# Moving a sketched linear attention and its MLP to 32x32 vector transposes, eight-tile float32 rounds, column-tiled kv and a list scheduler

## The chip, the cores and the metric

The kernel runs on one core of one Trainium2 chip. The metric is the device time of one execution in microseconds (us). The span that a profile shows is about 2 us shorter than the device time of the same run. The record calls a run slow when it is over 1.5% above the fastest of its kernel.

Engine names in the profiles: PE is TensorE's matmuls, PEld its weight loads, DVE is VectorE, ACT is ScalarE, POOL is GpSimd, SP is SyncE. A name with a q behind it (ACTq, SPq) is the engine's sequencer, which also issues DMAs.

## The reference

There are 4 batches, 4 heads, a sequence of 1088 and a head size of 32, so 4352 tokens of width 128. The MLP has 2048 hidden units.

```python
def phi(x):                                   # S1, S2: 8 x 32
    a = einsum('rd,bhsd->bhsr', S1, x)        # 8 numbers per token and head
    b = einsum('rd,bhsd->bhsr', S2, x)        # 8 more
    return outer(a, b).reshape(..., 64)       # 64 features
q_p, k_p = phi(q), phi(k)
kv  = einsum('bhsf,bhsd->bhfd', k_p, v)       # 64 x 32 per batch and head
z   = k_p.sum(axis=2)                         # 64 per batch and head
x   = (q_p @ kv) / (q_p . z + 1e-6)           # 4352 x 128
h   = x @ w_in                                # 128 x 2048
g   = maximum(h, 0) + alpha * minimum(h, 0)
out = g @ w_out                               # 2048 x 128
```

Both kernels rewrite the activation in the same way. Since min(h, 0) = h - relu(h), the output is x W + relu(h) w_a, with w_b = alpha * w_out, w_a = w_out - w_b and W = w_in w_b. These three are made on the chip once, after the weights have landed. So the first output matmul waits for w_in and w_out, and for a GpSimd product and difference.

## The kernel before

Everything except the hidden layer (bf16) is float32. A sequence of 1088 is 1024 plus a rest of 64, and rests of several batches are packed together. Work is written as short lists of steps. A merge by estimated cost interleaves the MLP of one batch with the queries of the next and the keys of the one after, and this fixes each engine's order.

```python
    def load_main(t, src, b):                  # one head at a time: 128-byte pieces
        for h in range(H):
            nc.sync.dma_start(t[:, :, h], bass.AP(..., ap=[[NJ * D, 128], [D, NJ], [1, D]]))
    ...                                        # cut: every load is issued by SyncE
    def k_feat(src, nj, ptag, store, abtag=None):
        ...                                    # transposes by TensorE, copy to kT
            nc.vector.tensor_mul(kp[:, :n], ...)         # outer product: VectorE, PSUM x SBUF
    ...
        def kv(kp_chunk, vt, rows, first, last):         # k features stationary, v moving
            for p in range(2):                           # two heads and the ones for z: 96 columns
                nc.tensor.matmul(acc["ps"][:, p], kp_chunk[rows, 2 * p:2 * p + 2]...,
                                 vt[rows, 3 * p:3 * p + 3], ...)
    ...
    def q_steps(srcs, col0, parts, ptag):      # half a batch: 512 tokens
        def tr():                              # four TensorE transposes, then a copy to qT
        ...
        def feat(S_):                          # two tiles (64 rows each) at once
            for p in range(2):
                nc.tensor.matmul(ps[:, p, :n], S_[64 * p:64 * (p + 1)]...,
                                 s["qT"][64 * p:64 * (p + 1), :n], start=True, stop=True)
        ...                                    # fa: Sa, copied by ScalarE; fb: Sb, multiplied by VectorE
        def nd():                              # two tiles at once, denominators, then numerators
            for o in (1, 0):
                for (b, c0, nn) in parts:
                    for p in range(2):
                        nc.tensor.matmul(ps[64 * p:64 * (p + 1), o, c0:c0 + nn], ...)
```

## Time and profile before

| | before |
|---|---|
| device time, median of 5 runs beside the changed kernel | 182.47 us (181.14 to 184.46) |
| span of the profiled run | 179.3 us |
| first hidden-layer matmul | 54.9 us (its own record is missing; its weights are loaded at 54.71) |
| last start on TensorE | 173.6 us |

These lines are from the page of the kernel before: the span, busy time with share and number of instructions per engine, then busy tenths in 40 slices of the span (9 is 90% or more), the clock that TensorE was granted in tenths, DMA rate per slice, and the shares of the chain of work that ended last.

```profile
span 179.3 us, 2240 instructions
...
PE 150.5 (84%) x817; PEld 82.9 (46%) x828; DVE 83.7 (47%) x152; ACT 79.6 (44%) x149; POOL 17.0 (9%) x35
...
PE   0160099999599999999999999999999999999970
...
GB/s 38 186 115 195 343 228 116 94 220 162 213 56 4 2 0 0 0 62 2 0 0 59 4 0 59 0 0 0 61 1 0 59 0 0 62 0 62 0 59 29
...
PE 79%; SPq 7%; DMA 5%; ACT 3%; DVE 2%; issue 2%; ACTq 0%
```

TensorE is full from the twelfth slice on (a slice is 4.5 us), and nothing else is near full. The first eleven slices are different: there the loads run, TensorE has holes, and no output is made. The table of windows of the kernel before says the same in numbers. Its columns are the window in us, its length, busy us (and instructions) of PE, PEld, DVE, ACT and POOL, the granted clock, the DMA share and GB/s.

```profile
0.00:20.00 20.00, 3.67 (x12) 2.29 (x12) 2.70 (x21) 2.32 (x4) 2.95 (x18) 1.00 0.71 155
20.00:40.00 20.00, 17.32 (x124) 16.12 (x124) 4.84 (x7) 5.58 (x11) 14.04 (x17) 1.00 0.89 187
...
80.00:100.00 20.00, 19.89 (x114) 11.18 (x114) 11.24 (x17) 10.93 (x20) 0.00 (x0) 1.00 0.04 15
```

In 80 to 100 us TensorE is busy 19.89 of 20 us, VectorE and ScalarE about 11. In the chain of waits of the kernel before (start, length, what), the longest single piece is the transfer of w_in:

```profile
14.44 8.18 DMA w_in_f<-in_moe_w_in_dram
```

What the parts to be changed cost is read from the timeline of the kernel before (start, length, engine, line, output<-inputs, shapes, count):

```profile
37.95 1.13 PE L308 MATMUL ps_w_339<-qT,Sa 64*128 64x512 f32 x4
...
43.79 1.94 PE L330 MATMUL ps_nd<-qp,kz_322 128*64 128x512 f32 x8
...
82.20 1.92 PE L261 MATMUL ps_kvz<-v_78,kp 128*128 128x96 f32 x16
```

A feature round of half a batch is one pair of tiles with 512 float32 columns in 1.13 us (recorded as four instructions, two per float32 matmul). Numerators and denominators take 1.94 us, and half of a batch's kv takes 1.92 us.

### The profile page before, as it was taken

The page shows a single profiled execution, that of the slowest core. Times are in us where ns is not written, and L with a number is a line of the kernel's source. Part 1 is how long each engine was busy: PE and PEld are TensorE (multiplying, and loading weights), DVE is VectorE, ACT ScalarE, POOL GpSimd, SP SyncE. Part 2 cuts the span into 40 slices and gives each one's busy share as a digit, 9 for nine tenths or more (in the row PEclk, how much of TensorE's full clock was granted, in tenths as well). Part 3 has the DMA queues.
Part 4 walks back from the last instruction along what each step waited for, and adds up shares of the span by engine and source line. Part 5 has one row for each costly group of instructions (what it writes and reads, how often), then busy time and mean ns, then how long its engine had stood idle before and what let it go on. Part 6 is the DMA issues. An engine that isn't in the chain of part 4 may idle for free.

```text
span 179.3 us, 2240 instructions
## 1 busy us (share of the span) xinstructions
PE 150.5 (84%) x817; PEld 82.9 (46%) x828; DVE 83.7 (47%) x152; ACT 79.6 (44%) x149; POOL 17.0 (9%) x35
## 2 busy tenths in 40 slices
PE   0160099999599999999999999999999999999970
PEld 0030099965263545456454554633333434355540
DVE  3010052115623662764558185454656647757740
ACT  2010051051126761755376285535635657657540
POOL 6000499600000000000000000000000000000000
PEclk9999999999999999999999999999999999999998
DMA  2968997599930000010001001000100100101011
GB/s 38 186 115 195 343 228 116 94 220 162 213 56 4 2 0 0 0 62 2 0 0 59 4 0 59 0 0 0 61 1 0 59 0 0 62 0 62 0 59 29
DMA packets 41050, 11.16 MB, mean 62 GB/s; under 512 B 37056, under 2 KB 39376, under 8 KB 40912
## 3 DMA queue, kind: packets, MB, share of 16 engines
q1 hardware_dynamic: 41040, 11.03, 27.4%
q8 instruction: 6, 0.10, 0.3%
q14 instruction: 4, 0.03, 0.1%
HBM read 8.80 MB, written 2.23 MB: 62 GB/s over the span
## 4 chain that ended last, share of the span: by engine, by line
PE 79%; SPq 7%; DMA 5%; ACT 3%; DVE 2%; issue 2%; ACTq 0%
PE ps_h L360 16%; PE ps_o L373 16%; PE ps_kvz L261 10%; PE ps_nd L330 9%; PE ps_ab L235 5%; DMA w_in_f<-in_moe_w_in_dram 5%; SPq L90 3%; PE ps_ot L391 3%; PE ps_qt L300 2%; PE ps_w L212 2%; PE ps_wt L203 2%; PE ps_kt L226 2%; DVE kp L243 1%; PE ps_o L372 1%; SPq L116 1%
## 5 line engine op out<-in xcount | busy, mean ns | idle before, releaser
L364 ACT ACTIVATE rh<-ps_h 128x512 bf16<-128x512 f32 (+1 forms) x98 | 53.5, 582 | 38.5 <-PE ps_h L360 35.9
L360 PE MATMUL ps_h<-xT,w_in_bf 128*128 128x512 bf16 (+1 forms) x139 | 48.6, 367 | 0.6 <-issue 0.2
L373 PE MATMUL ps_o<-rh,w_a_bf 128*128 128x512 bf16 (+1 forms) x138 | 47.3, 366 | 0.2
L366 DVE TENSOR_SCALAR rh<-ps_h 128x512 bf16<-128x512 f32 (+1 forms) x46 | 29.5, 647 | 14.6 <-PE ps_h L360 12.9
L360 PEld LDWEIGHTS <-w_in_bf 128*128 128x128 bf16 x144 | 14.2, 99 | 21.9 <-issue 11.9
L373 PEld LDWEIGHTS <-w_a_bf 128*128 128x128 bf16 x144 | 14.1, 98 | 14.4 <-issue 4.0
L335 DVE STREAM_TRANSPOSE dt<-ps_nd 128x512 f32<-128x512 f32 (+1 forms) x9 | 6.2, 687 | 18.2 <-PE ps_nd L330 18.2
L243 DVE TENSOR_TENSOR kp<-ps_ab,b_sb 128x1024 f32<-128x1024 f32 x8 | 9.8, 1224 | 9.4 <-ACT b_sb L75 9.4
L203 PE MATMUL ps_wt<-ident,w_in_f 128*128 128x128 f32 x16 | 3.9, 397 | 9.5 <-DMA w_in_f<-in_moe_w_in_dram 9.5
L235 PEld LDWEIGHTS ps_ab<-S12blk,kT 128*128 128x128 f32 x68 | 9.5, 211 | 5.1 <-ACT kT L75 2.8
L235 PE MATMUL ps_ab<-S12blk,kT 128*128 128x64 f32 x68 | 10.6, 298 | 1.0 <-ACT kT L75 1.0
L75 ACT COPY kT<-ps_kt 128x512 f32<-128x512 f32 (+1 forms) x9 | 4.7, 522 | 14.7 <-PE ps_kt L226 14.7
L196 POOL TENSOR_SCALAR w_b_f<-w_out_f,S12T_165 128x128 f32<-128x128 f32 x16 | 9.5, 616 | 16.7 <-DMA w_out_f<-in_moe_w_out_dram 16.7
L77 DVE COPY oT<-ps_ot 128x512 f32<-128x512 f32 (+1 forms) x8 | 5.3, 658 | 10.8 <-PE ps_ot L391 10.8
L203 PEld LDWEIGHTS ps_wt<-ident,w_in_f 128*128 128x128 f32 x16 | 3.0, 216 | 10.0 <-DMA w_in_f<-in_moe_w_in_dram 9.9
L75 ACT CAST w_in_bf<-w_in_f 128x512 bf16<-128x512 f32 x3 | 1.7, 615 | 10.7 <-DMA w_in_f<-in_moe_w_in_dram 10.7
L75 ACT COPY qT<-ps_qt 128x512 f32<-128x512 f32 (+1 forms) x9 | 5.2, 573 | 2.7 <-PE ps_qt L300 2.7
L340 DVE STREAM_TRANSPOSE rr<-rc 128x512 f32<-128x512 f32 (+1 forms) x9 | 6.1, 682 | 0.3
L75 ACT COPY b_sb<-ps_ab 128x128 f32<-128x128 f32 (+1 forms) x10 | 2.5, 251 | 7.9 <-PE ps_ab L235 7.9
L391 PE MATMUL ps_ot<-ident,ob 128*128 128x128 f32 x34 | 5.6, 281 | 0.5 <-ACT ob L75 0.5
L261 PE MATMUL ps_kvz<-v_77,kp 128*128 128x96 f32 x32 | 4.3, 282 | 2.0 <-DVE kp L243 2.0
L341 DVE TENSOR_TENSOR xT<-ps_nd,rr 128x512 bf16<-128x512 f32 (+1 forms) x9 | 5.9, 653 | 0.1
(148 smaller groups left out, 170.8 us busy)
## 6 DMA issues: line engine op xcount, KB each, us to landing
out_dram<-oT SPq DMA_DIRECT2D x8, 256.0 KB, 2.0
w_in_f<-in_moe_w_in_dram SPq DMA_DIRECT2D x1, 1024.0 KB, 8.2
k_68<-in_k_dram SPq DMA_DIRECT2D x4, 128.0 KB, 3.0
v_76<-in_v_dram SPq DMA_DIRECT2D x2, 256.0 KB, 3.0
q_72<-in_q_dram SPq DMA_DIRECT2D x4, 128.0 KB, 2.8
k_69<-in_k_dram SPq DMA_DIRECT2D x4, 128.0 KB, 6.6
v_77<-in_v_dram SPq DMA_DIRECT2D x2, 256.0 KB, 3.2
q_73<-in_q_dram SPq DMA_DIRECT2D x4, 128.0 KB, 3.6
```

The lines of the kernel that those rows point to most:

```text
L75: nc.scalar.copy(dst, src)
L196: nc.gpsimd.tensor_scalar_mul(w_b_f[:, c], w_out_f[:, c], alphaT[:, c:c + 1])
L203: nc.tensor.transpose(ps[:, c], w_in_f[:, (4 * i + c) * 128:(4 * i + c + 1) * 128], ident)
L235: nc.tensor.matmul(ps[:, j * H:(j + 1) * H], kT[:, j * 128:(j + 1) * 128], S12blk, start=True, stop=True)
L243: nc.vector.tensor_mul(kp[:, :n], bview(av, [list(av.ap[1]), list(av.ap[2]), [0, r]]), bview(bv, [list(bv.ap[1]), [0, r], list(bv.ap[2])]))
L261: nc.tensor.matmul(acc["ps"][:, p], kp_chunk[rows, 2 * p:2 * p + 2].rearrange("s h i j -> s (h i j)"), vt[rows, 3 * p:3 * p + 3], start=fi ...
L330: nc.tensor.matmul(ps[64 * p:64 * (p + 1), o, c0:c0 + nn], kvz_done[b][:, p, 64 * o:64 * (o + 1)], s["qp"][:, p, c0:c0 + nn], start=True, ...
L360: nc.tensor.matmul(ps[:, :n], w_in_bf[:, c * 128:(c + 1) * 128], xT[:, col0:col0 + n], start=True, stop=True)
L364: nc.scalar.activation(rh[:, :n], ps[:, :n], ACTF.Relu)
L366: nc.vector.tensor_scalar_max(rh[:, :n], ps[:, :n], 0.0)
L373: nc.tensor.matmul(s["o"][:, :n], w_a_bf[:, c], s["rh"].pop(c)[:, :n], start=False, stop=c == NC - 1)
L391: nc.tensor.transpose(ps[:, j], s["ob"][:, j * 128:(j + 1) * 128], ident)
```

## The change

The intent is to take work off TensorE, which is full for two thirds of the span, and to load faster at the start.

- Queries are transposed by VectorE in 32x32 blocks, straight from the loaded layout. The features then need 32 rows per head, so eight matmul tiles (4 row groups by 2 column groups) run in one round of 512 columns; numerators and denominators likewise use 2 row groups by 4 column groups. A batch takes four rounds of eight instead of eight rounds of two.
- kv has v stationary (32 columns per head) in four column tiles. The sum z comes from small products of a and b instead of ones beside v.
- Key products of batches 1 to 3 go to GpSimd; batch 0 and the rests stay on VectorE.
- Loads are in 1 KB pieces, issued by SyncE and ScalarE.
- A list scheduler with estimated durations orders every engine's work and picks the engine for the copies.

```diff
-        for h in range(H):
-            nc.sync.dma_start(t[:, :, h], ... [[NJ * D, 128], [D, NJ], [1, D]])
+        load(f"{name}{b}", eng, ..., ap=[[NJ * D, 128], [S * D, H], [1, NJ * D]])
...
+    load_main("k", k_sb, k, 0, "act")
+    load_main("q", q_sb, q, 0)
+    load_main("v", v_sb, v, 0, "act")
+    ...
+    load("w_in", "act", w_in_f, moe_w_in, 1 << 20)
+    load("w_out", "act", w_out_f, ...)
...
-            nc.tensor.transpose(ps[:, j * 128:(j + 1) * 128], c, ident)            # queries
+        nc.vector.transpose(bview(sb(bq), [[1, n]]), qsrc)                         # 32x32 blocks
...
-                nc.tensor.matmul(ps[:, p, :n], S_[64 * p:64 * (p + 1)], s["qT"][64 * p:64 * (p + 1), :n])
+        for t in range(4) if x is None else range(2 * x, 2 * x + 2):               # x: half a round
+            for c in range(2):
+                nc.tensor.matmul(ps(..)[64*c:64*c+64, t % 2, :nf], Sab[32*t:32*t+32, i], moving(.., t, c))
...
-                nc.tensor.matmul(acc["ps"][:, p], kp_chunk, vt)                    # 128x96
+                nc.tensor.matmul(ps(bk)[32*h:32*h+32, :R], v_sb[b][:, h, 4*hf+j], kp[:, h, j])  # 128x64
...
+    keys(0, at(0) - 16000, "dve")
+    for b in range(1, B): keys(b, ..., "pool")
+    done = plan(ops, classes)        # list scheduler: earliest start within 120 ns, then due time
```

In the changed kernel the first feature round (a) is one group of eight tiles. The second (b) is written as two groups of four that may stand apart in the order.

## The prediction

> **What bounds the kernel now.** Span 179.3 us (182.5 timed). From about 55 us to 173 us TensorE is the limit: it is busy 19.7 to 19.9 us in each 20 us window from 60 to 160 us, while VectorE and ScalarE are near 55% each; ScalarE's largest wait in the table of waits is for the hidden matmul (35.9 us). Before that the kernel is loading: TensorE does nothing from 14 to 22.6 us, and the chain of waits passes there through the w_in transfer (8.2 us). The first MLP matmul issues at 55 us. By start-to-start times in the timeline its work is about 136 us: MLP 60.5 (216 ns per matmul), queries 4.5 us per half batch (transposes 0.5, two feature rounds 1.06 each, numerator and denominator 1.87), 36 for eight and 2.5 for the rest; keys 6.6 per batch, 26; output transposes 5; weights 5.5.
>
> **What the change does on TensorE.**
> - A float32 round of 512 columns takes about 0.93 to 1.06 us with two tiles running at once. The change puts eight tiles in a round: four rounds per batch replace eight. The second feature round is split in two halves that sometimes stand apart, so I count 5 us per batch against 9. Saved: 16 us, and 0.8 on the rest. The Trainium skill, "TensorE: Matmul & The Clock Gate", Part 3, says tiles of distinct row and column groups run concurrently; the trace shows it for two tiles (eight records of about 0.6 us in 1.94 us), not yet for eight.
> - kv with v stationary: 48 small matmuls. The remainder denominators here issue a record every 26 ns, so 96 records take an estimated 2.5 us, against 4.0; the extra transposes return 0.5. Saved: about 4.
> - Query transposes leave TensorE (counted).
> Estimated total: 116 us.
>
> **Other engines.** VectorE loses six 1.22 us key products to GpSimd (estimate 2.3 us each from 4.5 us for 2048 elements) but gains query transposes (4 x 1.25, estimated) and small fix-ups; I get about 86 us VectorE, 80 us ScalarE. So TensorE stays the limit.
>
> **Start.** Packets of 128 bytes become 1 KB and two queues issue; the skill's "DMA: Bandwidth & Descriptors", Specifications, asks for at least 512 B; in this trace the rate was 114 to 150 GB/s in small packets and 355 in the weights' stretch. At about 270 GB/s shared by both queues, w_in lands near 18 us, w_out near 25, and GpSimd then needs 6.8 us for w_b and the first half of w_a. First MLP matmul about 28 us, outputs flow from about 32.
>
> **Sum.** From 32 us about 100 us of TensorE work are left; 5% for stalls (a fixed order, 1.25 us VectorE pieces, three hidden-layer banks) makes 105; the tail is 4 to 5 us as now. Span about 140, timed 143 us.
>
> Range 132 to 156. Faster 0.97, same 0.02, slower 0.01.
>
> **Right if:** first MLP matmul near 28 us; a round of eight takes 1.0 to 1.2 us; kv block 2 to 3 us; TensorE at least 93% busy after 35 us; VectorE and ScalarE each 55 to 65%.
>
> **Wrong if:** eight float32 tiles do not overlap (about 2 us a round: +14 us); loads of later batches hold back w_out, and with it every output matmul; kv stands in TensorE's order waiting for GpSimd, whose queue holds w_b and w_a ahead of the key products; the planned order mismatches real durations and TensorE idles on the hidden banks.

## The result, and the profile after

The changed kernel took 156.16 us (155.64 to 158.17, 5 runs) against 182.47 us. The ratio of fast runs is 0.857, with a 95% interval of 0.851 to 0.863. A ratio here is the mean time of one kernel's fast runs over that of the other's of the same rounds, so it is not quite the ratio of the medians quoted. The change is 14% faster, and 13 us slower than predicted.

The first profile of the changed kernel fell in the slow state, so the profile shown is that of the same kernel run again (e0_again below), a fast run. Its page:

```profile
span 154.4 us, 2980 instructions
...
PE 124.4 (81%) x1230; PEld 65.6 (42%) x1230; DVE 89.6 (58%) x148; ACT 74.5 (48%) x140; POOL 21.4 (14%) x15
...
PE   0305771975799997999999999999999999999920
...
GB/s 114 405 320 345 277 284 364 174 0 0 4 0 0 4 0 0 70 2 4 0 72 0 0 4 68 0 20 52 0 0 41 31 0 68 4 68 2 68 9 27
...
PE 73%; DVE 8%; ACT 6%; DMA 6%; issue 2%; SPq 1%; ACTq 1%
```

The loads end in the eighth slice (a slice is 3.86 us), at about 30 us, where they had lasted into the twelfth slice, about 50 us, before. But TensorE has holes up to the eleventh slice. VectorE and ScalarE, 2% and 3% of the chain before, now have 8% and 6%. The windows of the changed kernel, columns as before:

```profile
10.00:20.00 10.00, 5.46 (x23) 4.77 (x23) 3.11 (x3) 3.90 (x8) 0.24 (x1) 1.00 1.12 312
...
30.00:41.00 11.00, 7.21 (x81) 4.13 (x73) 7.75 (x10) 2.52 (x3) 0.00 (x0) 1.00 0.01 2
...
80.00:100.00 20.00, 19.78 (x164) 8.56 (x155) 15.05 (x27) 11.74 (x21) 0.21 (x1) 1.00 0.04 15
```

From 30 to 41 us no data is being loaded (2 GB/s), TensorE is busy 7.21 of 11 us, and no hidden matmul has run yet. That window is where the prediction had outputs flowing. After that, TensorE is as full as before (19.78 of 20).

Three stretches add up to the span. The first ends at the first hidden-layer work, the second at TensorE's last start, and the third is the last copy and store.

| stretch | before | predicted | after |
|---|---|---|---|
| start to first hidden matmul | 54.9 | 28 | 41.4 |
| from there to the last start on TensorE | 118.7 | 109 | 106.3 |
| tail | 5.7 | 4.5 | 6.7 |
| span | 179.3 | 141.5, rounded to 140 | 154.4 |

The predicted 109 us are from 28 us to the end of 32 + 105 = 137 us. So the middle term was right within 3 us. The error before the first hidden matmul, 13.4 us, is as large as the whole miss (12.9 us against 141.5), since the errors of the other two terms nearly cancel.

What the middle stretch consists of is found by giving each group of TensorE instructions the time from its start to the next group's start. With the groups that the table leaves out, both columns sum to the stretch; the work is not quite the same, since the kernel before had already made more of its keys, of its first queries and W when the stretch began.

| us of TensorE, start to start | before | after |
|---|---|---|
| query features, numerators, denominators, transposes | 33.8 | 17.1 |
| kv and z sums | 8.3 (2 batches) | 4.4 (3 batches) |
| hidden and output matmuls, and x W | 66.7 | 69.8 |
| W itself | 0 (made at 30 us) | 3.74 |

The four rows leave out key transposes and features, output transposes and the last small steps of the keys (11.3 us after). In the query work after, the first feature round (57.21 us) took 1.54 us instead of 1.11, because its last four tiles waited for W to be copied out of its PSUM bank. The query work is halved: three batches and the rest in 17.1 us, about 5.1 us per batch, as predicted (5). kv takes 1.46 us per batch, less than the predicted 2.5. The timeline of the changed kernel shows both:

```profile
49.98 0.65 PE L409 MATMUL ps<-kp__72,v 128*32 128x64 f32 x32
...
60.16 1.09 PE L466 MATMUL ps<-qT__75,Sab 32*64 32x512 f32 x8
...
61.94 1.09 PE L466 MATMUL ps<-qT__75,Sab 32*64 32x512 f32 x8
...
64.83 1.09 PE L492 MATMUL ps<-aq__77,zc 64*32 64x512 f32 x16
```

Eight float32 tiles of 512 columns (x16 records) take 1.09 us, where one pair of tiles took 1.13 us before. The page "TensorE: Matmul & The Clock Gate", Part 3, of the Trainium skill says that tiles of distinct row and column groups run concurrently, and this trace agrees for eight. It also shows what the split of the second round costs: each group of four (x8 records) takes 1.09 us as well, so the two halves cost two rounds.

Now the start. The chain of waits of the changed kernel (start, length, what), from the first load to the first feature round of the queries, has these pieces:

```profile
1.89 8.69 DMA q<-in_q_dram
10.66 0.82 ACTq L215
11.52 1.28 ACT L194
12.81 0.59 ACT kT__64 L194
13.45 1.97 PE ps L366 x8
...
20.75 3.59 DVE kpr L379
...
28.48 1.94 PE ps L466 x16
```

L215 is the line that issues loads, and ACTq is ScalarE's sequencer. ScalarE does nothing until 10.6 us, loads its function table (1.28 us), and makes its first copy at 12.81 us. The table of waits of the changed kernel names what it waited for, in front of the issue of w_out:

```profile
ACT w_out_f L215 <- DMA q<-in_q_dram: 10.6, 1, 10.6
```

Nothing in the data asks for this: w_out has nothing to do with q. In the instruction records of the trace the loads use eight completion semaphores again and again (numbers 100 to 107), and the issue of w_out waits for number 104, the one that q's first load had. It therefore waits until that load has landed, and ScalarE's copies stand behind it in ScalarE's order. The timeline of the changed kernel shows what was ready meanwhile, and two more oddities:

```profile
4.98 1.09 PE L359 MATMUL ps<-ident,k 128*128 128x128 f32 x4 [4.98 <-DMA k<-in_k_dram]
...
10.61 1.25 DVE L459 STREAM_TRANSPOSE qT__74<-q 128x1024 f32<-128x1024 f32 x1 [3.60 <-DMA q<-in_q_dram]
...
19.76 4.29 POOL L310 TENSOR_TENSOR w_b_f<-w_out_f,S12T 128x2048 f32<-128x2048 f32 x1 [18.45 <-DMA w_out_f<-in_moe_w_out_dram]
...
20.75 3.58 DVE L379 TENSOR_TENSOR kpr<-abr 128x256 f32<-128x256 f32 x1
...
28.41 2.01 PE L466 MATMUL ps<-qT__74,Sab 32*64 32x512 f32 x16
...
40.06 1.10 PE L366 MATMUL ps<-S12blk,kT__64 128*128 128x64 f32 x8 [0.72 <-ACT kT__64 L194]
...
41.44 0.59 PE L565 MATMUL ps<-xT__95,w_in_bf 128*128 128x512 bf16 x2
...
70.66 0.43 DVE L379 TENSOR_TENSOR kpr<-abr 128x256 f32<-128x256 f32 x1
```

- The keys' transposes are done at 6 us and wait 6.7 us for ScalarE's copy.
- The transposed queries are ready at 11.86 us, but their first feature round starts at 28.41 us, since kv stands ahead of it in TensorE's order.
- A VectorE product of 256 columns (kpr, the key features of the packed rests, L379) takes 3.58 us beside a GpSimd product. The same instruction for the second pair of rests, at 70.66 us in this run, where GpSimd does nothing, takes 0.43 us.
- A group of key features takes 1.97 us at 13.45 us and 1.10 us at 40.06 us, and the query round at 28.41 us takes 2.01 us. TensorE ran at about half speed there. The clock row of the page shows 9 in these slices; the clock's own record in the trace has no entry before 31.9 us, where it grants full speed for the first time (27.9 us in the kernel before).

### The profile page after: what moved, and what is told of

Same layout as the page of the kernel before. It is cut to its first block, busy times and chain, and to the rows that moved or that the text cites. A ratio compares the mean times of both kernels' runs of the same rounds, so it can differ in the third digit from the quotient of the medians.

```text
span 156.2 us, 2980 instructions
## 1 busy us (share of the span) xinstructions
PE 127.2 (81%) x1230; PEld 66.5 (43%) x1230; DVE 89.5 (57%) x148; ACT 74.5 (48%) x140; POOL 21.5 (14%) x15
## 4 chain that ended last, share of the span: by engine, by line
PE 74%; DVE 8%; ACT 6%; DMA 6%; issue 2%; SPq 1%; ACTq 1%; DVEq 0%
PE ps L583 20%; PE ps L565 18%; PE ps L466 8%; PE ps L366 7%; DMA q<-in_q_dram 6%; PE ps L492 5%; PE ps L600 3%; PE ps L359 3%; PE ps L341 2%; DVE kpr L379 2%; PE ps L409 2%; PE ps L329 2%; DVE aq__76 L479 1%; PE ps L579 1%; PE ps L439 1%
## 5 line engine op out<-in xcount | busy, mean ns | idle before, releaser
L565 PE MATMUL ps<-xT__95,w_in_bf 128*128 128x512 bf16 x64 | 25.5, 405 | 0.0
L565 PEld LDWEIGHTS <-w_in_bf 128*128 128x128 bf16 x144 | 14.5, 100 | 13.9 <-issue 4.0
L565 PE MATMUL ps<-xT__96,w_in_bf 128*128 128x512 bf16 (+1 forms) x48 | 15.4, 343 | 0.2
L571 ACT ACTIVATE rh__82<-ps 128x512 bf16<-128x512 f32 (+1 forms) x17 | 9.8, 575 | 6.4 <-PE ps L565 6.4
L573 DVE TENSOR_SCALAR rh__87<-ps 128x512 bf16<-128x512 f32 x10 | 6.9, 692 | 8.3 <-PE ps L565 7.6
L571 ACT ACTIVATE rh__84<-ps 128x512 bf16<-128x512 f32 (+1 forms) x14 | 7.9, 567 | 7.6 <-PE ps L565 7.3
L565 PE MATMUL ps<-xT__97,w_in_bf 128*128 128x512 bf16 x32 | 11.5, 379 | 0.0
L366 PE MATMUL ps<-S12blk,kT__64 128*128 128x64 f32 x32 | 5.2, 316 | 7.7 <-ACT kT__64 L194 7.7
L573 DVE TENSOR_SCALAR rh__89<-ps 128x512 bf16<-128x512 f32 x13 | 8.9, 687 | 3.3 <-PE ps L565 3.1
L359 PE MATMUL ps<-ident,k 128*128 128x128 f32 x32 | 6.1, 323 | 5.7 <-DMA k<-in_k_dram 5.1
L571 ACT ACTIVATE rh__88<-ps 128x512 bf16<-128x512 f32 (+1 forms) x16 | 9.2, 572 | 3.0 <-PE ps L565 2.9
L573 DVE TENSOR_SCALAR rh__85<-ps 128x512 bf16<-128x512 f32 (+1 forms) x10 | 6.6, 661 | 4.8 <-PE ps L565 4.8
L571 ACT ACTIVATE rh__86<-ps 128x512 bf16<-128x512 f32 (+1 forms) x13 | 7.5, 580 | 3.4 <-PE ps L565 3.2
L379 POOL TENSOR_TENSOR kp__72<-ab__69 128x1024 f32<-128x1024 f32 x2 | 3.9, 1952 | 34.0 <-ACT ab__69 L194 34.0
L466 PE MATMUL ps<-qT__74,Sab 32*64 32x512 f32 (+1 forms) x96 | 7.9, 580 | 0.1
L571 ACT ACTIVATE rh__83<-ps 128x512 bf16<-128x512 f32 (+1 forms) x10 | 5.8, 579 | 4.4 <-PE ps L565 4.3
L583 PE MATMUL ps<-rh__82,w_a_bf 128*128 128x512 bf16 (+1 forms) x18 | 6.9, 383 | 1.0 <-DVE ob__90 L196 0.8
L573 DVE TENSOR_SCALAR rh__83<-ps 128x512 bf16<-128x512 f32 (+1 forms) x8 | 5.3, 658 | 3.2 <-PE ps L565 3.1
L466 PE MATMUL ps<-qT__75,Sab 32*64 32x512 f32 x64 | 7.0, 613 | 0.1
```

Of the source, the lines that this page charges most:

```text
L359: nc.tensor.transpose(ps(bt)[:, j * 128:(j + 1) * 128], s, ident)
L366: nc.tensor.matmul(ps(bf)[:, j * 64:(j + 1) * 64], sb(bT)[:, j * 128:(j + 1) * 128], S12blk.rearrange("p h c -> p (h c)"), start=True, sto ...
L379: (nc.vector if e == "dve" else nc.gpsimd).tensor_tensor(out=dst, in0=i0, in1=i1, op=ALU.mult)
L466: nc.tensor.matmul(dst, bview(Sab[32 * t:32 * t + 32, i], [[1, R]]), moving(sb(bq), t, c), start=True, stop=True)
L565: nc.tensor.matmul(ps(b)[:, :n], w_in_bf[:, c * 128:(c + 1) * 128], xs(), start=True, stop=True)
L571: nc.scalar.activation(sb(br)[:, :n], ps(b)[:, :n], ACTF.Relu)
```

## The experiments

Twelve runs were made (the first is the changed kernel again). All gave right results. Only e1, e2 and e7 keep TensorE's order, instruction by instruction, and e8 keeps that of e4; in the other runs the list scheduler also moved other work, so there the edit and the new order act together. The ratios are to the kernel before, run in the same rounds. "First h" is the start of the first hidden-layer matmul, the end of the first stretch above. The theory at the outset was that the lost 13 us lie in the start: ScalarE held by the issue of w_out, VectorE held by GpSimd, and the fixed order on TensorE. The rivals were that it is a matter of the clock, or of the middle stretch (the split round, GpSimd's key products).

### e0_again: the changed kernel, once more

There is no edit. It gives the fast profile and the spread on the same chip as the next three.

> The changed kernel once more, on this chip, as the yardstick of the runs beside it. Ratio to the kernel before 0.85 to 0.865; span 154 us in the fast state, 156 us when the TensorE clock is halved[...]; first hidden matmul at about 41 us.

Measured: 156.78 us (156.05 to 158.06), ratio 0.855 [0.845, 0.864], span 154.4 us, first h 41.44 us. The result repeats. What the slow profile added can be seen here too: in the slow profile the clock's record falls to half speed from 40.4 us for 6.83 us, and in that stretch hidden matmuls were spaced 426 ns instead of 216 ns. The page of that slow run (slice 11 and 12 are the stretch):

```profile
PEclk9999999999659999999999999999999999999995
```

So the fall of the clock costs some runs 2 us more. That it comes from the idle TensorE of 30 to 41 us is argued, not shown: the fast run has the same holes and no fall. The Trainium skill, "TensorE: Matmul & The Clock Gate", Part 1, says that TensorE's clock is halved when it was idle and is judged in free-running windows of 3413 ns; 6.83 us is two such windows, so this trace agrees with the length of the window.

### e1_wout_sync: w_out issued by SyncE

```diff
-    load("w_out", "act", w_out_f, ...)
+    load("w_out", "sp", w_out_f, ...)
```

TensorE's, VectorE's and GpSimd's orders are unchanged, instruction by instruction.

> One word changed: the w_out load is issued by SyncE instead of ScalarE; the order of every other instruction is the same. Theory A (ScalarE is held from 2.3 to 10.6 us by a load that waits for an earlier one, and the whole start hangs on its first copy): the first ScalarE copy comes at 6 to 7 us instead of 12.8, the key product of the remainder is over before GpSimd starts on w_b and takes 0.43 us instead of 3.58, the first hidden matmul issues at 31 to 32 us instead of 41, and the span falls by 9 to 10 us to about 144.5. Theory B (the start is bound by the arrival of q, k, v and the remainders through two queues that share the engines): first hidden matmul within 2 us of 41, span 152 or more. Theory C (the miss lies in the MLP phase): span unchanged within 1 us even if the first hidden matmul moves.

Measured: 148.72 us (147.9 to 151.53), ratio 0.810 [0.797, 0.823], span 146.1 us, 8.3 us less than e0_again, and first h 33.19 us, 8.25 us less. The whole gain is in the start. The timeline of this kernel:

```profile
6.03 0.59 ACT L194 COPY kT__64<-ps 128x512 f32<-128x512 f32 x1 [2.44 <-PE ps L359]
...
14.16 0.42 DVE L379 TENSOR_TENSOR kpr<-abr 128x256 f32<-128x256 f32 x1
...
14.67 3.61 POOL L310 TENSOR_TENSOR w_b_f<-w_out_f,S12T 128x2048 f32<-128x2048 f32 x1 [13.37 <-DVE kpr L379]
...
19.88 3.94 DVE L196 CAST w_in_bf<-w_in_f 128x512 bf16<-128x512 f32 x3
...
33.19 0.59 PE L565 MATMUL ps<-xT__95,w_in_bf 128*128 128x512 bf16 x2
```

ScalarE's first copy now waits for TensorE alone and starts at 6.03 instead of 12.81 us. kpr comes before GpSimd's product and takes 0.42 us. w_out lands at about 14.5 instead of 19.6 us, so the edit does two things at once (ScalarE freed, w_out earlier), and no run separates them. But before the first hidden matmul only GpSimd's w_b and w_a read w_out, so its landing can act there only through the work that GpSimd holds up on VectorE. Taking the largest such hold away alone gave 2.5 us (e2), so ScalarE is the main one: an estimated 5.7 of the 8.25 us (8.25 less 2.5). The casts of w_in on VectorE took 1.11 and 2.58 us beside GpSimd's w_a, and 0.42 us for the third, which starts at 23.41 us, when GpSimd is done (23.20); e7 asks whether that matters.

### e2_rest_psum: the kpr product reads one input from PSUM

```diff
         def pr(e):
             i0 = bview(a, [[r, m], [1, r], [0, r]])
+            if tag == "kr0":                                   # the first rest alone
+                i0 = bview(ps(bf), [[2 * r, m], [1, r], [0, r]])
...                                                             # cut: the PSUM tile is held until then
```

> Only the remainder key product of batch 0 takes one of its two inputs from PSUM instead of SBUF; the order is the same and GpSimd still works on w_b at that moment. Theory A2 (a VectorE instruction with two SBUF inputs is held while GpSimd runs one): the product takes 0.4 to 0.5 us instead of 3.58, the first hidden matmul comes 3 us earlier, at about 38, span about 151. Rival (its length has another cause, such as a late semaphore or the small tile): it still takes 3 us or more and the span stays within 1 us of 154.

Measured: 155.07 us (153.72 to 156.34), ratio 0.838 [0.826, 0.849]; the fast runs are 153.72 and 153.8 us. Span 151.9 us, 2.5 us less than e0_again; first h 38.91 us, 2.5 us less. The timeline of this kernel:

```profile
19.73 4.28 POOL L310 TENSOR_TENSOR w_b_f<-w_out_f,S12T 128x2048 f32<-128x2048 f32 x1 [18.43 <-DMA w_out_f<-in_moe_w_out_dram]
...
20.71 0.42 DVE L381 TENSOR_TENSOR kpr<-ps,abr 128x256 f32<-128x256 f32 x1
```

The same product, started at the same time beside the same GpSimd instruction, takes 0.42 us when one of its inputs is in PSUM, and 3.58 us when both are in SBUF; and with both in SBUF it takes 0.43 us when GpSimd does nothing (70.66 us in e0_again). So it needs both, the two SBUF inputs and the GpSimd product beside it. In e0_again it ended within 0.3 us of GpSimd's w_b (24.33 and 24.05 us). The Trainium skill says so in "GPSIMD Engine Reference", 1. Specifications: GpSimd's SBUF interfaces are "Shared with VectorE (contention with DVE instructions in a 2-port perf mode or with two SBUF inputs)". The trace agrees, and the prediction had not used it. In the kernel before, kpr read one input from PSUM, the form that e2 goes back to, so it is the change that opened it to this hold.

### e3_q_first: the first query round ahead of the keys' later steps

```diff
-    x[0] = q_main(0, at(0) - 15900)
+    x[0] = q_main(0, at(0) - 15985, at(0) - 15900)     # due time of the feature rounds; of the rest
...                                                        # cut: the second due time is passed on
```

> Only the priority of the first batch's query features is raised, so that both feature rounds stand in TensorE's order before the keys' kv block instead of after it. Theory A3 (the fixed order keeps ready query features, whose input is transposed at 11.8 us, behind the kv block until 28.4): first feature round at about 19 us, first hidden matmul at 36 to 37, span about 149.5. Theory B: no earlier, because the inputs of the kv block set the time; span 153 or more.

Measured: 156.2 us (153.2 to 156.47), but three of the four runs, the profiled one too, are slow, so there is no ratio. The one fast run took 153.2 us (span 151.4), 3 us less than e0_again's fast profile. First h is 38.73 us in the slow profile, 2.7 us less than e0_again's, and 2.1 us less than in the slow profile of the changed kernel (40.81), which is the like pair; 36 to 37 had been expected. The round moved to 18.82 us as meant, but ran cold: 2.50 us, and 2.90 us for the second, against 1.09 us warm. One fast run is thin, but the first h points the same way.

### e4_start_all: e1, e2 and e3 together

The edits are those of the three kernels above.

> All three edits of the start together: w_out issued by SyncE, the remainder product reading PSUM, the query features of batch 0 ahead of the kv block. Theory A (these waits stand one behind another): first hidden matmul at 30 to 32 us, span 143 to 145. If they only mask one another, it is no better than the w_out edit alone (33.2 us, span 146.1). The three casts of w_in on VectorE fall beside GpSimd's w_a and should take about 3.9 us together instead of 1.05.

Measured: 148.29 us (146.65 to 150.16), ratio 0.805 [0.796, 0.813], span 145.0 us, first h 31.65 us. The three alone took 8.25, 2.5 and 2.1 to 2.7 us off the start, about 13 us; together they take 9.8 us, which is 1.5 us more than e1 alone. They are not independent: e1 alone already brings kpr out of GpSimd's way (0.42 us there), so e2's gain is inside e1's.

### e5_b_whole: the second feature round as one group of eight

```diff
-        for x in range(2):
-            bo_.append(op("pe", ..., rnd(1, b2, x), [o], [bq, b2[x]], ..., due + 4 + x / 2, tag + "b"))
+        bw_ = op("pe", nf * 1.7 + 150, rnd(1, b2), [o], [bq] + b2, 200, due + 4, tag + "b")
+        bo_ = [bw_, bw_]
```

> Only the second feature round is issued as one group of eight matmuls instead of two groups of four that the scheduler may place apart. If a group of four costs a full round (1.02 us by the start-to-start times), each of four batches gives back about 1 us: span 150.5 to 152 against 154.4. If the group of eight has to wait in TensorE's order for the second ScalarE copy (1.0 us), the gain is lost again: span 153.5 to 155.

Measured: 152.75 us (152.45 to 154.64), ratio 0.840 [0.832, 0.848], span 151.0 us. First h is unchanged (41.36 us), and the middle stretch is 102.9 instead of 106.3 us. Query features of the three batches, start to start, take 6.52 us, which is 1.09 us for each of six rounds, instead of 9.68 us for three whole rounds and six halves. The timeline of this kernel:

```profile
56.66 1.11 PE L466 MATMUL ps<-qT__75,Sab 32*64 32x512 f32 x16
...
60.05 1.11 PE L466 MATMUL ps<-qT__75,Sab 32*64 32x512 f32 x16
```

Eight tiles cost what four cost. Writing a round as two groups wastes half of it each time they are not neighbours in TensorE's order: 3.2 of the 3.4 us are the query features.

### e6_keys_vector: all key products on VectorE

```diff
-        keys(b, at(2 * b) - LEAD - 6000, "pool")
+        keys(b, at(2 * b) - LEAD - 6000, "dve")
```

> The key products of batches 1 to 3 go back from GpSimd to VectorE; the scheduler may place things anew. Theory A (TensorE is the limit after the start): VectorE gains about 7.3 us of work (six products of 1.22 us), to about 97 us of the span, and the span stays within 1.5 us of 154.4. Rival (freeing VectorE was a main source of the gain): the span grows by 3 us or more.

Measured: 157.12 us (155.66 to 157.67), ratio 0.853 [0.837, 0.870], span 154.9 us, the middle stretch 105.8 us. The page of this kernel:

```profile
PE 123.9 (80%) x1216; PEld 65.7 (42%) x1230; DVE 96.4 (62%) x155; ACT 74.0 (48%) x139; POOL 9.7 (6%) x9
```

VectorE takes the 6.8 us back (96.4 instead of 89.6) and nothing becomes longer within the spread. First h is 1.0 us later (42.44 us) and the middle stretch 0.5 us shorter. GpSimd's key products neither help nor hurt here, since VectorE has room: it is not what TensorE waits for in the middle stretch.

### e7_casts_scalar: e1, with the casts of w_in on ScalarE

```diff
-        c_win.append(op(("act", "dve"), {"act": 615, "dve": 350}, wc, ...))
+        c_win.append(op("act", {"act": 615, "dve": 350}, wc, ...))
```

> The w_out edit, and the casts of w_in fixed to ScalarE; TensorE's order is that of the w_out edit alone. Theory A2 (VectorE work [...]is held by GpSimd's two-input instructions: three casts took 3.94 us beside w_a): VectorE's 3.9 us there vanish, the casts take 0.63 us each on ScalarE, and the first hidden matmul comes 1 to 3 us before 33.2, the smaller figure if the copies of the query features on ScalarE then set the time. Span 143.5 to 145. Rival (the casts were slow by themselves): they stay slow on ScalarE and nothing moves.

Measured: 147.8 us (147.4 to 149.54), ratio 0.813 [0.803, 0.822], span 146.1 us as in e1; first h 33.12 against 33.19 us. The 3.9 us of VectorE are gone and nothing is gained: the expectation missed. The query product that follows on VectorE still starts at 25.45 us (25.54 in e1). The casts were slow, but not on the path; a slow instruction is not yet a cost. The record shows another hold, which this edit left in place. A VectorE product of only 32 columns with both inputs in SBUF runs beside GpSimd's w_b in e1 and in e7 (the line is from e7's timeline):

```profile
16.74 1.63 DVE L433 TENSOR_TENSOR fs__98<-fs__98,mask 128x32 f32<-128x32 f32 x1
```

It takes 0.19 us in e8, after GpSimd's work, and TensorE waits 2.45 us for the copy behind it.

### e8_best: e1, e2, e3 and the casts on ScalarE

The edits are those shown above, with no other.

> The three start edits and the casts on ScalarE: the version that the theory points to. First hidden matmul at 28 to 30 us, where the prediction had put it, and a span of 141 to 143 us, timed 143 to 145: then the start is the whole of the miss. If the span stays above 146 while the first hidden matmul comes at 30, the MLP phase was mis-sized as well.

Measured: 146.9 us (146.34 to 150.04), ratio 0.805 [0.798, 0.811], span 145.1 us, first h 31.69 us. It equals e4 (145.0 and 31.65), so the expectation, a span of 141 to 143 us and first h at 28 to 30, missed. The casts on ScalarE gain nothing here either.

### e9_best_whole: e8 with the whole second round

The edits are those of e8 and e5.

> The start edits together with the undivided second feature round. The two act in different stages, so they should add: first hidden matmul near 31.7 us, and 103 us instead of 106.5 from there to the last matmul, span 141.5 to 142.5, timed 143 to 144.5. If they get in each other's way, 144 or more.

Measured: 145.15 us (144.88 to 145.52), ratio 0.789 [0.783, 0.796], span 143.6 us, first h 32.47 us, the middle stretch 104.4 us. The two fixes add only in part, 1.5 us instead of e5's 3.4, and the expectation of 141.5 to 142.5 us missed. Two things can be seen. First, the first of the six later rounds took 2.64 us to the next instruction instead of e5's 1.27 (query features 7.87 us in all instead of 6.5):

```profile
48.50 1.54 PE L468 MATMUL ps<-qT__75,Sab 32*64 32x512 f32 x16
...
51.14 0.38 PE L585 MATMUL ps<-rh__82,w_a_bf 128*128 128x512 bf16 x1 [1.10 <-DVE ob__90 L196]
```

The clock's record grants full speed from 24.2 to 140.25 us, so this is no half speed: the round's last four tiles started 0.48 us behind the others, as they waited for W to be copied out of its PSUM bank, and then TensorE waited 1.10 us for a copy by VectorE. Second, first h is 0.8 us later than in e8. There TensorE's new order puts twelve transposes of w_in (2.77 us) ahead of the kv block, where e8 has four, and kv starts at 22.80 instead of 21.14 us.

### e10_warm: e9 with eight idle matmuls at the start

```diff
+    b_warm = Buf("po")
+    def warm(e):
+        for _ in range(8):
+            nc.tensor.matmul(ps(b_warm)[:, :128], ident, ident, start=True, stop=True)
+    op("pe", 3400, warm, [c_id], [b_warm], 200, due=-8.5e5, name="warm")
```

They run while TensorE waits for the first keys; their result is not used.

> As the run before it, with eight matmuls of the identity by itself put on TensorE while it waits for the first keys; their result is never read. If the slow early matmuls (groups of four key features take 1.97 us at 10 us and 1.10 at 30 us; the first feature rounds 2.0 to 2.9 us against 1.06 later) are slow because TensorE has just been idle, they shorten to 1.1 and about 1.1 us and the first hidden matmul comes 2 to 4 us earlier, span 138.5 to 140.5. If the cause is another, they stay and the span does not change by 1 us.

Measured: 143.06 us (142.01, 142.94 and 143.17 in fast runs, 145.9 in a slow one), ratio 0.776 [0.765, 0.787], span 140.1 us, first h 30.44 us, 2.0 us less than e9. The timeline of this kernel:

```profile
7.43 1.10 PE L373 MATMUL ps<-S12blk,kT__64 128*128 128x64 f32 x8 [0.68 <-ACT kT__64 L194]
...
14.95 2.90 PE L475 MATMUL ps<-qT__74,Sab 32*64 32x512 f32 x16 [1.10 <-ACT aq__76 L194]
...
30.44 0.38 PE L574 MATMUL ps<-xT__95,w_in_bf 128*128 128x512 bf16 x1
```

The first group of key features takes 1.10 us instead of 1.97, so the clock was the reason for the doubled times. But the query rounds took 2.02 and 2.90 us, since the clock's record falls to half speed again from 9.96 to 20.2 us. So this was partly confirmed. What the clock was worth is not separated. Of the 2.0 us, 1.7 lie before the kv block, which starts at 21.12 instead of 22.80 us. There the edit also changed TensorE's order: transposes of w_in now fill its waits around the keys of the rests, and e8, without any warm-up, has its kv block at 21.14 us. In the profiled runs the middle stretch fell too, from 104.4 to 103.0 us, as the first later round took 1.27 us again instead of 2.64.

### e11_warm_gaps: e10 with more idle matmuls behind each early group

```diff
+            if tag.startswith("k0"):
+                idle(3)          # three matmuls of the identity behind each early key group
...
+                if tag == "q0":
+                    idle(6)      # six behind each feature group of batch 0's queries
```

> As the run before it, with three to six more of the idle identity matmuls behind each group of the first keys and of the first query features, so that TensorE has no long gap until the kv block. Theory (what is left of the start's delay is TensorE at half clock): the second group of key features stays at 1.1 us, the first batch's two feature rounds take about 1.1 us each instead of 2.0 and 2.9, the first hidden matmul comes at 27.5 to 29 us, where the prediction had put it, and the span at 137 to 139. If the clock is granted for another reason than activity, the rounds stay slow and the extra matmuls only delay them: span 140 or more.

Measured: 142.35 us (142.2 to 142.38 in fast runs, 144.45 in the slow, profiled one). There is no ratio, since too few of the runs of the kernel before were fast beside it. The timeline of this kernel, from the slow run:

```profile
13.44 1.11 PE L483 MATMUL ps<-qT__74,Sab 32*64 32x512 f32 x16
...
30.65 0.63 PE L584 MATMUL ps<-xT__95,w_in_bf 128*128 128x512 bf16 x1
```

The query rounds now take 1.11 and 1.64 us at the start too, and the clock's record is at full speed from 9.54 to 30.02 us, so here the extra activity did hold the clock. First h, at 30.65 us, does not move, because the idle matmuls cost about what the clock gives back: the two rounds start 1.6 and 1.1 us later than in e10 (13.44 and 16.02 instead of 11.84 and 14.95 us), and the second ends at 17.66 instead of 17.85 us. The fast spans are 140.4 to 140.6 us, e10's are 140.1 to 141.4 us. So the first warm-up with its new order is worth 2 us, and more of it nothing.

## Why the prediction was right or wrong

**The direction and the middle stretch were right.** TensorE was the limit, and the change removed about what was predicted. The query work fell to 5.1 us per batch (predicted 5), eight tiles overlap fully (1.06 to 1.11 us a round, predicted 1.0 to 1.2), and kv fell to 1.46 us (predicted 2 to 3, so too high). From the first hidden matmul to the last start on TensorE 109 us were predicted and 106.3 measured. That sum is better than its terms, so part of it is luck: the hidden and output matmuls took 69.8 us from start to start where 60.5 and 5 for stalls had been predicted, and kv of three batches 4.4 where 7.5 had. VectorE's share was 58%, inside the predicted 55 to 65%; ScalarE's, 48%, was below it. Of the things listed under "wrong if", unoverlapped tiles did not come. kv did not wait for GpSimd's key products: with them on VectorE (e6) the time is the same. It did stand behind GpSimd's w_b, but through VectorE's product of the rests (item 2 below). The idle on hidden banks is inside the middle stretch, which was shorter than predicted. w_out was in fact held back by a load, but by an earlier one (q's first) through its semaphore, not by later ones through the bandwidth. "TensorE at least 93% busy after 35 us" holds only from 41 us on (19.78 of 20 us in the window shown).

**The step that failed is "Start": "First MLP matmul about 28 us, outputs flow from about 32".** Measured were 41.4 us and 43.4 us (the first output matmul). This term of the sum was mis-sized by 13.4 us, and the sum's total error in span is 154.4 - 140 = 14.4 us: 13.4 from the start, 2.2 from the tail, -2.7 from the middle and 1.5 from rounding 141.5 to 140.

The prediction sized the start by the arrival of data. That part was too slow, not too fast: it had w_in at 18 and w_out at 25 us, and they landed at about 9.2 and 19.6 us, with 273 to 312 GB/s in the first 20 us where 270 had been assumed. The "DMA: Bandwidth & Descriptors" page was used for the size of a piece, and the trace agrees that 1 KB pieces run faster than 128-byte ones did (155 GB/s in the first 20 us of the kernel before), though two queues issue now and the two were not separated. What the prediction did not ask is what each engine does between its data and the first hidden matmul. The runs showed this in its place:

1. **A DMA issue on a compute engine's queue held that engine: up to 8.3 us.** ScalarE could not issue w_out before q's first load had landed, because of a reused completion semaphore, and its copies stood behind. Shown by e1: one word changed, 8.25 us off first h, 8.3 us off the span. How much of it is ScalarE freed and how much w_out landing 5.1 us sooner was not separated by a run; an estimated 5.7 us is ScalarE (8.25 less the 2.5 of e2), and the chain names ScalarE.
2. **GpSimd's weight products held VectorE: 2.5 us.** A VectorE product with both inputs in SBUF took 3.58 instead of 0.42 us. Shown by e2, and by the same instruction without GpSimd beside it (0.43 us). It lies inside item 1's gain, since e1 moves the product ahead of GpSimd's. The same kind of hold on the casts (3.94 us) cost nothing (e7).
3. **TensorE's order: 2.1 to 2.7 us alone, 1.5 on top of item 1.** The query round stood ready for 16.5 us behind kv. Read from e3's first h in a slow profile and one fast run, which is thin, and from e4, where the three together gave 9.8 us against e1's 8.25.
4. **The clock: some part of 2 us.** The early groups ran at half speed, at 1.97 instead of 1.10 us. That the clock was the reason is shown by e10 and e11; what it cost is not, since e10's 2.0 us come with a new order on TensorE. The durations in the prediction were read where TensorE had long been busy (and the clock row shows full speed at the start, where nothing was recorded), so it had priced cold work warm.

With all of these first h is at 30.4 us. What remains against 28, 2.4 us, is probably the serial chain of the first queries (product, denominators, transposes, reciprocal, product), which takes 5.6 us in e11 from the first denominators at 25.05 us to the first hidden matmul. No run takes it apart, so this is argued and not shown.

**The tail** was predicted at 4 to 5 us "as now" and measured at 6.7 us (5.7 before). The last store takes 5.8 us from its issue to the end of the span, against 4.7 us before. It was not tested.

**The best version** is e10 with e11 beside it: 143.06 and 142.35 us, 0.776 of the kernel before for e10. That e10's time is the predicted 143 us is a coincidence: it is the time of another kernel, without those holds and with the undivided second round of e5, its first h is still 30.4 us and not 28, and its middle stretch is 103 us and not 109.

## What to carry to other kernels

When a change makes loads faster, price the start as a chain of instructions on each engine, not as the arrival of the last byte: look for a DMA issue that stands in a compute engine's queue ahead of its first work (10.6 us here), and for VectorE instructions with two SBUF inputs beside a long GpSimd instruction (3.58 instead of 0.42 us here). Take durations for the start from the start, where TensorE may be at half speed, even when the clock row shows nothing (1.97 instead of 1.10 us here). Write matmuls that can share a round of tiles as one group, since here four tiles cost what eight did (1.09 us). When a scheduler orders the work, compare the orders of two kernels before giving the difference to the edit. And before mending a slow instruction, check that something waits for it.

## What the Trainium skill lacked or had wrong

- "DMA: Bandwidth & Descriptors" (Anatomy of one DMA) says that a semaphore wait happens on the issuing sequencer before dispatch. It lacks what follows for a kernel: such a wait on ScalarE's queue also stops ScalarE's compute behind it. Here the issue of w_out waited until 10.6 us for the completion of an unrelated load, whose semaphore it reuses, and moving the issue to SyncE (e1) took 8.3 us off the span.
- "TensorE: Matmul & The Clock Gate", Part 1, says that matmul starts are never closer than about 25 ns. Column-tiled kv (128x32 stationary, 64 columns, float32, four column groups) starts 32 records in 0.47 us, 49.98 to 50.45 us in e0_again, which is 15 ns each: four tiles start 7 ns apart, and a new four starts every 56 ns. So the sentence needs an exception for tiles of distinct column groups; Part 3 of the same page has it, with starts about 4 ns apart.
- The same page, Part 1, has the half clock of an idle start, and the runs agree (1.97 against 1.10 us; a fall of 6.83 us, two windows). The page does not say that a profile's clock row can show full speed before the clock's first record, at 31.9 us here.
